# Weight conversion, softmax denominators and tile buffers: a change of operand places, engines and order in an attention and MLP kernel

## The chip, the cores and the metric

The kernel runs on one core of one Trainium2 chip. The metric is the device time of one execution in microseconds. The core's engines work side by side, each through its own instructions in order: TensorE (PE in the profile; PEld are its weight loads), VectorE (DVE), ScalarE (ACT), GpSimd (POOL), and SyncE (SP), which here only issues DMA transfers. Engines wait for each other by semaphores. SBUF is the on-chip memory that the engines read and write; PSUM is the smaller memory into which TensorE writes its products, and which DVE and ACT can read and write too.

## The reference: what is computed

Attention over a sliding window of 128 with a distance bias per head, then two matrix products with the mish activation between them:

```python
B, H, S, D = 8, 8, 576, 64
scores = q @ k.T / sqrt(D)
scores = where((rel >= 0) & (rel < 128), scores - slope[h] * |rel|, -1e9)   # rel = i - j
attn = exp(scores - max(scores))
attn = attn / (sum(attn) + 1e-9)
x = (attn @ v).transpose(0, 2, 1, 3).reshape(B * S, H * D)      # 4608 x 512
h = x @ w_in                                                    # 4608 x 2048
out = (h * tanh(log1p(exp(h)))) @ w_out                         # 4608 x 512
```

The inputs q, k and v are float32. The two weight matrices reach the chip as the bits of float64 numbers, as pairs of 32-bit words.

## The kernel before, in words

**Batches and stages.** The 4608 tokens are worked in nine chunks of 512: chunk c < 8 is the first 512 tokens of batch c, and the ninth chunk gathers the last 64 tokens of every batch. Ahead of the loop comes the attention of batch 0 with the conversion of three weight tiles (the "first attention"). Then each turn c of the loop has two stages. Stage 1 computes h = x @ w_in in eight steps j of 24 products (`first`, 192 products `h` in all) and applies mish on ACT (`mish`, tile `g`). Stage 2 computes g @ w_out (`second`, products `po`) and, mixed with it, the attention of the next batch.

**Precision.** Each operand of the two large products is split into an upper and a lower part in fp32r, and three products are made of them. `split_x` splits x (ACT copies, DVE subtracts), `parts` splits g into tile `gg` (ACT copies, POOL subtracts), and `convert_w` splits the weights into `si` and `so`.

**Weight conversion.** There are 16 weight tiles: eight of w_in (`wi`) and eight of w_out (`wo`), each 128 x 2048 words, in the order of the list `conv`. A conversion has four steps. `scaled` (line 147): ACT scales the upper words, read as float32, into tile `t` (`ti`, `to` in the profile); where `sign` is set ACT also replaces the upper words by their sign. `joined` (line 159): DVE shifts and joins the bits. Where `sign` is set, two operations of 1024 elements write into `t`, and POOL multiplies by the sign; otherwise three operations of 1024 elements write the float32 value over the upper words. `upper` (line 194): ACT copies the value into the upper part. `lower` (line 198): POOL subtracts. In the run before, three weights are converted with the sign in the first attention, ten without it in stage 1 of turn 0, and three with it in stage 2 of turn 0.

**Attention.** A batch has four pairs of heads, and each pair two units (`unit`, line 260) of two blocks of 128 rows, and one last unit (`last_unit`, line 365) for the last 64 rows, with an `l` behind the pair's number in names. A unit makes scores `s` on PE into PSUM; DVE adds the bias and ACT takes the exponential, with sums in `sm` (tile `pz`); `fold` adds the two halves on POOL and takes the reciprocal of the sums on DVE; `scale` multiplies by it; PE transposes the weights into PSUM; DVE multiplies them by the triangular `masks`; PE multiplies with v (`o`). In a last unit, the DVE does fold and scaling too, and the result is copied to tile `xo` and stored to `xs` in DRAM through SP's queue, for the ninth chunk. The tile pool `at` has two buffers of a tile unless told otherwise, and so `xo` has two.

**Order.** Every engine works in program order (`InOrder`, lines 20 to 32; the profile therefore shows line 30 for nearly all instructions). The program order is written by hand: each step has a due time, steps of a stage are sorted by it and written out. Stage steps have due times in units of j, attention steps in units of one unit's number k, and a conversion has one due time for each of its four steps (lines 560 to 597). SP's queue holds, in this order, the loads of batch 0, the loads of sixteen halves of `wi` and fourteen of `wo`, and then the stores of `xo` and the loads of batch 1.

Of the kernel before, what the change touches and what calls it, by code (L numbers as in the profile page):

```python
# [35 lines left out]
def attention_mish_mlp(  # L36
# [38 lines left out]

    nb = const.tile([P, H, 2 * WINDOW], BF16, tag="nb", name="nb")
# [10 lines left out]


    masks = const.tile([P, 2, P], BF16, tag="masks", name="masks")
    make_lower_triangular(nc, masks[:, 0, :], diag=False)  # L90
    make_upper_triangular(nc, masks[:, 1, :])
# [5 lines left out]
    zero = const.tile([P, 1], U32, tag="zero", name="zero")  # L97
    pool.memset(zero, 0)
# [7 lines left out]
    def big(name, dtype):  # L106
        return wts.tile([P, 2048], dtype, tag="w", name=name, bufs=2 * NJ + NF // 4)
# [29 lines left out]
    def convert_w(kind, j, sign):  # L137
# [9 lines left out]
        def scaled():  # L147
            st["w"] = split[(kind, j)] = big(f"s{kind}{j}", F32R)
            if not bits:
                return  # L150
            st["t"] = t = ff.tile([P, 1024], F32, tag="gg", name=f"t{kind}{j}", bufs=3)
            for a, raw in enumerate(parts_):
                val = raw[:, 1::2].bitcast(F32)

                act.activation(t[:, a * n : (a + 1) * n], val, AF.Copy, scale=2.0**-112)
                if sign:
                    act.activation(val, val, AF.Sign)

        def joined():
            if not bits:  # L160
                return
            for a, raw in enumerate(parts_):
                low, high = raw[:, 0::2], raw[:, 1::2]
                t = st["t"][:, a * n : (a + 1) * n]
                tb = t.bitcast(U32)
                out_ = tb if sign else high
# [8 lines left out]
                if sign:
                    val = high.bitcast(F32)
                    pool.tensor_tensor(out=val, in0=t, in1=val, op=ALU.mult)
                else:
                    dve.scalar_tensor_tensor(
                        out=high, in0=tb, scalar=0x80000000, in1=high, op0=ALU.bitwise_and,  # L180
                        op1=ALU.bitwise_or,
                    )
# [19 lines left out]
        return scaled, joined, upper, lower  # L202
# [57 lines left out]
    def unit(b, p, half):  # L260
# [43 lines left out]
        def fold():  # L304
            sm, pz = st["sm"], st["pz"]
            two = pz if half else pz[:, 1:4:2]
            pool.tensor_tensor(out=two[:, :, :P], in0=two[:, :, :P], in1=two[:, :, P:], op=ALU.add)
            dve.scalar_tensor_tensor(
                out=sm, in0=sm, scalar=1e-9, in1=sm, op0=ALU.add, op1=ALU.max
            )  # L310
            dve.reciprocal(sm, sm)

        def scale():
            (pool if b == 0 else dve).tensor_tensor(
                out=st["pz"][:, :, :P], in0=st["pz"][:, :, :P],
                in1=st["sm"].rearrange("p (c n) -> p c n", n=1).to_broadcast([P, 4, P]), op=ALU.mult,
            )
# [47 lines left out]
    def last_unit(b, p):  # L365
# [45 lines left out]
        def values():  # L411
# [8 lines left out]
            xo = at.tile([P, LEFT], F32, tag="xo", name=f"xo{name}")  # L420
# [73 lines left out]
    po = {}  # L494
# [171 lines left out]
```

## Time and profile before

| what | us |
|---|---|
| median of 3 runs | 1073.17 (1072.72 to 1073.31) |
| the profiled execution's own time | 1073.7 |
| its span, first to last instruction | 1072.0 |
| first attention, 0 to | 83.6 |
| stage 1 of turn 0 | 83.6 to 139.2 |
| stage 2 of turn 0 | 139.2 to 225.8 |
| turn 1 (both stages) | 225.8 to 337.1 |
| PE busy, whole span | 1007.2 (94%) |
| DVE, ACT, POOL busy | 433.4, 389.1, 325.1 |

Rows of the profile name an instruction as "output tile <- input tiles", with the shape, partitions x elements; a number in brackets at the end of a row is the idle time of the engine ahead of it, and what ended that idle time. A matmul row gives rows*columns of the array, then the moving shape. The granted clock is the share of full TensorE speed that the profile records in a stretch.

### The profile page before, as it was taken

The numbers are of one execution on the slowest core, as the hardware profiler recorded it, in microseconds if no ns is written. First come the engines' busy times: TensorE is split into PE (matmuls) and PEld (weight loads), VectorE is DVE, ScalarE is ACT, GpSimd is POOL, SyncE is SP. The second block draws the span as 40 slices with busy tenths as digits, with TensorE's granted clock in tenths as the row PEclk, the third lists the DMA queues.
The fourth block names the chain that finished last, engine by engine and source line by source line (L and its number), as shares of the span: only waits on it lengthen the run. The fifth ranks groups of instructions, "written<-read, shape, count | busy, mean of one in ns | idle before, by whom it ended". The sixth has DMA issues, their size and how long they took to land.

```text
span 1072.0 us, 14004 instructions
## 1 busy us (share of the span) xinstructions
PE 1007.2 (94%) x5280; PEld 792.4 (74%) x5280; DVE 433.4 (40%) x1114; ACT 389.1 (36%) x903; POOL 325.1 (30%) x263
## 2 busy tenths in 40 slices
PE   5639867999999999999999999999999999999998
PEld 3427655788777877787778777877788778888886
DVE  4668987710663056304740275017600771010000
ACT  3435564512542154314431443235323452231121
POOL 3335567310341044203420333024401440041042
PEclk9989889999999999999999999999999999999999
DMA  8940011210122003200320022002200201010001
GB/s 271 398 158 1 0 63 36 86 37 1 53 65 67 1 26 92 67 1 25 90 68 1 24 73 65 23 2 70 82 31 1 61 33 41 1 40 20 1 1 40
DMA packets 52131, 59.30 MB, mean 55 GB/s; under 512 B 13024, under 2 KB 32608, under 8 KB 52064
## 3 DMA queue, kind: packets, MB, share of 16 engines
q1 hardware_dynamic: 50880, 57.69, 16.7%
q8 instruction: 42, 0.69, 0.3%
q10 hardware_dynamic: 1184, 0.72, 0.2%
q14 instruction: 25, 0.20, 0.1%
HBM read 47.91 MB, written 10.49 MB: 54 GB/s over the span
## 4 chain that ended last, share of the span: by engine, by line
PE 85%; DVE 7%; issue 4%; POOL 2%; ACT 1%; DMA 1%; POOLq 0%; ACTq 0%; DVEq 0%
PE po L30 37%; PE h L30 33%; PE s L30 9%; PE o L30 5%; DVE wo L30 2%; DVE wi L30 2%; DVE pz L30 1%; DVE to L30 1%; POOL pz L30 1%; DMA nb<-in_relb_dram 1%; ACT pz L30 1%; POOL so L30 0%; DVE pz_2l L30 0%; POOL gg L30 0%; DMA first<-in_k_dram 0%
## 5 line engine op out<-in xcount | busy, mean ns | idle before, releaser
L30 PE MATMUL po<-so,gg 128*128 128x512 f32 x1728 | 433.1, 401 | 0.2 <-POOL gg L30 0.2
L30 PE MATMUL h<-x,si 128*128 128x512 f32 x1728 | 398.0, 392 | 4.8 <-ACT g L30 4.8
L30 POOL TENSOR_TENSOR gg<-g,gg 128x512 fp32r<-128x512 f32 x144 | 188.6, 1313 | 652.3 <-ACT gg L30 584.9
L30 PEld LDWEIGHTS h<-x,si 128*128 128x128 f32 x1728 | 326.8, 189 | 73.8 <-ACT g L30 5.5
L30 PEld LDWEIGHTS po<-so,gg 128*128 128x128 f32 x1728 | 317.2, 190 | 74.1 <-ACT x L30 6.6
L30 DVE CUSTOM_DVE_ANT_0 pz<-s,nb 128x256 f32<-128x256 f32 (+1 forms) x256 | 84.6, 386 | 303.2 <-PE s L30 293.6
L30 ACT ACTIVATE pz<-pz,mx 128x256 f32<-128x256 f32 (+1 forms) x256 | 120.4, 471 | 180.8 <-DVE mx L30 180.8
L30 ACT ACTIVATE g<-h 128x1024 f32<-128x1024 f32 x72 | 73.9, 1026 | 267.4 <-PE h L30 267.4
L30 ACT ACTIVATE gg<-g 128x512 fp32r<-128x512 f32 x144 | 88.5, 621 | 46.6 <-PE po L30 46.6
L30 DVE TENSOR_TENSOR pz<-s,masks 128x1024 f32<-128x1024 f32 x64 | 78.3, 1223 | 24.9 <-PE s L30 24.9
L30 DVE TENSOR_TENSOR pz<-pz,sm 128x512 f32<-128x512 f32 x56 | 55.7, 994 | 59.9 <-POOL pz L30 59.9
L30 POOL TENSOR_TENSOR pz<-pz 128x256 f32<-128x256 f32 x64 | 64.3, 1005 | 26.3 <-ACT pz L30 26.3
L30 PE MATMUL s<-ident,pz 128*128 128x128 f32 x256 | 43.4, 297 | 24.3 <-POOL pz L30 14.1
L30 PE MATMUL s<-qk 64*128 64x128 f32 (+1 forms) x448 | 58.4, 380 | 3.8 <-ACT g L30 3.8
L30 PEld LDWEIGHTS s<-ident,pz 128*128 128x128 f32 x256 | 34.2, 152 | 35.6 <-POOL pz L30 16.3
L30 DVE COPY ob<-po 128x512 f32<-128x512 f32 x18 | 12.4, 692 | 117.5 <-PE po L30 117.5
L30 PE MATMUL o<-pz,va 128*64 128x128 f32 (+1 forms) x560 | 54.9, 325 | 1.6 <-DVE pz L30 1.6
L30 PEld LDWEIGHTS o<-pz,va 128*64 128x64 f32 x560 | 33.3, 136 | 29.6 <-issue 12.0
L30 ACT ACTIVATE x<-o 128x512 fp32r<-128x512 f32 x32 | 19.1, 596 | 85.9 <-PE o L30 85.9
L30 ACT ACTIVATION_READ_ACCUMULATOR pz<-pz,mx 128x1 f32 x256 | 47.9, 187 | 0.0
L30 PEld LDWEIGHTS s<-qk 64*128 64x128 f32 x448 | 34.4, 188 | 15.0 <-issue 8.2
L30 DVE SCALAR_TENSOR_TENSOR sm<-sm 128x4 f32<-128x4 f32 x64 | 36.3, 568 | 12.5 <-ACT pz L30 12.5
(121 smaller groups left out, 521.5 us busy)
## 6 DMA issues: line engine op xcount, KB each, us to landing
wi<-in_moe_w_in_dram SPq DMA_DIRECT2D x16, 512.0 KB, 10.1
wo<-in_moe_w_out_dram SPq DMA_DIRECT2D x16, 512.0 KB, 10.2
out_dram<-ob SPq DMA_DIRECT2D x32, 256.0 KB, 2.0
qk<-in_q_dram SPq DMA_DIRECT2D x28, 288.0 KB, 3.7
qk<-in_k_dram SPq DMA_DIRECT2D x28, 288.0 KB, 4.0
va<-in_v_dram SPq DMA_DIRECT2D x28, 256.0 KB, 2.9
first<-in_q_dram SPq DMA_DIRECT2D x4, 288.0 KB, 3.9
first<-in_k_dram SPq DMA_DIRECT2D x4, 288.0 KB, 4.3
```

The costliest lines, as they stand in the source:

```text
L30: return self.tc.keep_in_program_order(method(*args, **kwargs))
```

## The change

It has eight parts. (1) `masks` is built first on POOL. (2) The tile `zero` is gone: in conversions with the sign (now called `early`) the first DVE operation is a tensor_scalar on one tensor in SBUF, where it was a scalar_tensor_tensor with the broadcast zero. (3) Conversions of stage 1 are done in two halves of 512: ACT writes the scaled words into PSUM (tiles `t` under the tags po0 and po1), DVE shifts them from PSUM to PSUM (tiles `u`, tags w and o), and two more DVE operations have one operand in SBUF and one in PSUM. That is six DVE operations of 512 for one weight, where there were three of 1024. (4) Three, nine and four weights are converted in the first attention, stage 1 and stage 2, where it was three, ten and three; due times are new. (5) Denominators of a unit are written into a free part of its scores in PSUM, and `scale` runs on DVE for batch 0 too, where it ran on POOL. (6) In a last unit the add moves from DVE to POOL and the scaling from DVE to ACT. (7) `xo` has four buffers. (8) Products of the masks with themselves, 128 x 256 in bf16, are written to a PSUM tile `idle` that nothing reads: 18 ahead of the first attention, four and eight in each of its units.

```diff
-    def convert_w(kind, j, sign):
+    def convert_w(kind, j, early):
...
+            if not early:
+                t = st[a] = ps.tile([P, 512], F32, tag=f"po{a}", name=f"t{kind}{j}_{a}")
+                act.activation(t, halves[a][:, 1::2].bitcast(F32), AF.Copy, scale=2.0**-112)
+                return
...
+            if not early:
+                low, high, tb = halves[a][:, 0::2], halves[a][:, 1::2], st[a].bitcast(U32)
+                u = ps.tile([P, 512], F32, tag=("w", "o")[a], name=f"u{kind}{j}_{a}").bitcast(U32)
+                dve.tensor_scalar(
+                    out=u, in0=tb, scalar1=3, scalar2=None, op0=ALU.logical_shift_left
+                )
+                dve.scalar_tensor_tensor(
+                    out=high, in0=low, scalar=29, in1=u, op0=ALU.logical_shift_right,
+                    op1=ALU.bitwise_or,
+                )
+                dve.scalar_tensor_tensor(
+                    out=high, in0=tb, scalar=0x80000000, in1=high, op0=ALU.bitwise_and,
+                    op1=ALU.bitwise_or,
+                )
+                return
...
-                dve.scalar_tensor_tensor(
-                    out=out_, in0=tb, scalar=3, in1=zero.to_broadcast([P, n]), op0=ALU.logical_shift_left,
+                dve.tensor_scalar(
+                    out=tb, in0=tb, scalar1=3, scalar2=None, op0=ALU.logical_shift_left
+                )
...
-            dve.scalar_tensor_tensor(
-                out=sm, in0=sm, scalar=1e-9, in1=sm, op0=ALU.add, op1=ALU.max
-            )
-            dve.reciprocal(sm, sm)
+
+            r = st["r"] = st["s"][:, 1, :4]
+            dve.tensor_scalar(out=r, in0=sm, scalar1=1e-9, scalar2=None, op0=ALU.add)
+            dve.reciprocal(r, r)
 
         def scale():
-            (pool if b == 0 else dve).tensor_tensor(
+            dve.tensor_tensor(
...
-            dve.scalar_tensor_tensor(
-                out=sm, in0=sm, scalar=1e-9, in1=sm, op0=ALU.add, op1=ALU.max
-            )
-            dve.reciprocal(sm, sm)
-            dve.tensor_tensor(out=pz[:, :64], in0=pz[:, :64], in1=pz[:, P:], op=ALU.add)
-            dve.tensor_scalar(out=pz[:, :P], in0=pz[:, :P], scalar1=sm, scalar2=None, op0=ALU.mult)
+            pool.tensor_tensor(out=pz[:, :64], in0=pz[:, :64], in1=pz[:, P:], op=ALU.add)
+            r = st["s"][:, 1, 4:5]
+            dve.tensor_scalar(out=r, in0=sm, scalar1=1e-9, scalar2=None, op0=ALU.add)
+            dve.reciprocal(sm, r)
+            act.activation(pz[:, :P], pz[:, :P], AF.Copy, scale=sm)
...
-            xo = at.tile([P, LEFT], F32, tag="xo", name=f"xo{name}")
+            xo = at.tile([P, LEFT], F32, tag="xo", name=f"xo{name}", bufs=4)
...
+    idle = ps.tile([P, 512], F32, tag="po0", name="idle")
+
+    def busy(n):
+        for _ in range(n):
+            pe.matmul(
+                idle[:, : 2 * P], lhsT=masks[:, 0, :], rhs=masks.rearrange("p u n -> p (u n)"),
+                start=True, stop=True,
+            )
+
+    def stages(*times):
+        t, d, u, low = times
+        return t, t + 0.01, d, d + 0.01, u, low
+
     early = attention(0) + converting(
-        conv[:3], [(4.3, 4.8, 5.6, 5.7), (5.5, 6.35, 7.1, 7.2), (7.0, 8.1, 8.7, 8.8)], True
+        conv[:3],
+        [stages(4.3, 4.85, 5.6, 5.7), stages(5.5, 6.4, 7.1, 7.2), stages(7.0, 8.1, 8.7, 8.8)], True,
     )
+    for k in range(2 * NP):
+        early += [(k + 0.015, lambda: busy(4)), (k + 1.35, lambda: busy(8))]
...
+    busy(18)
     run(early)
...
-            starts = [-0.5 + 0.78 * n for n in range(10)]
+            starts = [-0.5 + 0.84 * n for n in range(9)]
             steps += converting(
-                conv[3:13], [(t, t + 0.3, t + 1.1, t + 1.15) for t in starts], False
+                conv[3:12], [(t, t + 0.42, t + 0.3, t + 0.72, t + 1.15, t + 1.2) for t in starts], False
             )
...
-                conv[13:], [(0.5, 1.5, 3.5, 3.6), (2.5, 3.6, 5.5, 5.6), (6.0, 7.0, 9.0, 9.1)], True
+                conv[12:],
+                [
+                    stages(0.3, 1.2, 2.8, 2.9), stages(2.0, 3.0, 4.8, 4.9),
+                    stages(4.0, 5.0, 6.8, 6.9), stages(7.0, 8.0, 10.0, 10.1),
+                ],
+                True,
             )
```

Where the instructions stand: DVE at the start of stage 1 of turn 0, just behind the last unit of the first attention (`pz_3_1` is pair 3, half 1; the number behind a name tells buffers apart). Before:

```order
L30 TENSOR_TENSOR pz_3_1_508<-s_3_1_491,masks 128x2x4x128
L30 TENSOR_TENSOR x_3_575<-o_3_537,x_3_575 128x512
L30 SCALAR_TENSOR_TENSOR wi_148<-ti_597,zero 128x1024
L30 SCALAR_TENSOR_TENSOR wi_148<-wi_148 128x1024
L30 SCALAR_TENSOR_TENSOR wi_148<-ti_597,wi_148 128x1024
```

The same place with the change:

```order
L30 TENSOR_TENSOR pz_3_1_605<-s_3_1_584,masks 128x2x4x128
L30 TENSOR_TENSOR x_3_688<-o_3_642,x_3_688 128x512
L30 TENSOR_SCALAR ui_0_712<-ti_0_710 128x512
L30 SCALAR_TENSOR_TENSOR wi_146<-wi_146,ui_0_712 128x512
L30 SCALAR_TENSOR_TENSOR wi_146<-ti_0_710,wi_146 128x512
L30 TENSOR_SCALAR ui_1_718<-ti_1_716 128x512
L30 SCALAR_TENSOR_TENSOR wi_146<-wi_146,ui_1_718 128x512
L30 SCALAR_TENSOR_TENSOR wi_146<-ti_1_716,wi_146 128x512
```

Three operations of 1024 have become twice three of 512; `ti` and `ui` are in PSUM now.

ACT in the first attention, around the last unit of pair 2 (`pz_2l`); `ti` and `wi` belong to the first weight converted there. Before:

```order
L30 ACTIVATE ti_366<-wi_139 128x1024
L30 ACTIVATE wi_139<-wi_139 128x1024
L30 ACTIVATE pz_2l,sm_2l<-pz_2l,mx_2l 128x192
L30 ACTIVATE x_1_396<-o_1_330 128x512
L30 ACTIVATE pz_2_1_401,sm_2_1_400<-pz_2_1_401,mx_2_1_399 128x256 x4
```

With the change:

```order
L30 ACTIVATE ti_427<-wi_137 128x1024
L30 ACTIVATE wi_137<-wi_137 128x1024
L30 ACTIVATE pz_2l,sm_2l<-pz_2l,mx_2l 128x192
L30 ACTIVATE pz_2l<-pz_2l,sm_2l 128x128
L30 ACTIVATE x_1_469<-o_1_387 128x512
L30 ACTIVATE pz_2_1_474,sm_2_1_473<-pz_2_1_474,mx_2_1_472 128x256 x4
```

The scaling of the last unit stands ahead of the copy of x and of the next unit's exponentials. It needs POOL's add and DVE's reciprocal.

POOL in stage 2 of turn 0, where weights of w_out are converted beside the attention of batch 1 (`pz` rows are its folds, `gg` the lower parts of g). Before:

```order
L30 TENSOR_TENSOR gg_0_4_969<-g_2_756,gg_0_4_969 128x512
L30 TENSOR_TENSOR pz_0_1_954<-pz_0_1_954 128x4x128
L30 TENSOR_TENSOR so_932<-wo_181,so_932 128x2x512
L30 TENSOR_TENSOR gg_0_5_1002<-g_2_756,gg_0_5_1002 128x512
L30 TENSOR_TENSOR wo_0_869<-to_1012,wo_0_869 128x512
L30 TENSOR_TENSOR wo_1_870<-to_1012,wo_1_870 128x512
L30 TENSOR_TENSOR gg_0_6_1065<-g_3_833,gg_0_6_1065 128x512
L30 TENSOR_TENSOR pz_1_0_1039<-pz_1_0_1039 128x2x128
```

With the change:

```order
L30 TENSOR_TENSOR gg_0_4_1137<-g_2_911,gg_0_4_1137 128x512
L30 TENSOR_TENSOR so_1097<-wo_176,so_1097 128x2x512
L30 TENSOR_TENSOR wo_179<-to_1151,wo_179 128x1024
L30 TENSOR_TENSOR pz_0_1_1127<-pz_0_1_1127 128x4x128
L30 TENSOR_TENSOR gg_0_5_1177<-g_2_911,gg_0_5_1177 128x512
L30 TENSOR_TENSOR so_1150<-wo_179,so_1150 128x2x512
L30 TENSOR_TENSOR gg_0_6_1236<-g_3_997,gg_0_6_1236 128x512
L30 TENSOR_TENSOR wo_0_1037<-to_1222,wo_0_1037 128x512
L30 TENSOR_TENSOR wo_1_1038<-to_1222,wo_1_1038 128x512
L30 TENSOR_TENSOR pz_1_0_1208<-pz_1_0_1208 128x2x128
L30 TENSOR_TENSOR pz_1l<-pz_1l 128x64
```

Between the fold of the second unit (`pz_0_1`) and that of the third (`pz_1_0`) there is a whole weight's pair of operations more ahead of it, and the add of the last unit has joined.

More of the change, by code (lines that the diff above doesn't have):

```diff
@@ L74, in attention_mish_mlp @@
     nc.scalar.preload_act_table_set("exp_and_others")
+    masks = const.tile([P, 2, P], BF16, tag="masks", name="masks")
+    make_lower_triangular(nc, masks[:, 0, :], diag=False)
+    make_upper_triangular(nc, masks[:, 1, :])
     nb = const.tile([P, H, 2 * WINDOW], BF16, tag="nb", name="nb")
@@ L86, in attention_mish_mlp @@
         nc.gpsimd.memset(t[64:P], 0.0)
-    masks = const.tile([P, 2, P], BF16, tag="masks", name="masks")
-    make_lower_triangular(nc, masks[:, 0, :], diag=False)
-    make_upper_triangular(nc, masks[:, 1, :])
     xs = dram.tile([NCC, P, CH], F32, tag="xs", name="xs")
@@ L96, in attention_mish_mlp @@
     )
-    zero = const.tile([P, 1], U32, tag="zero", name="zero")
-    pool.memset(zero, 0)
     bits = w_in.dtype != F32
@@ L145, in convert_w, with scaled @@
         st = {}
-        def scaled():
-            st["w"] = split[(kind, j)] = big(f"s{kind}{j}", F32R)
+        def scaled(a):
+            if a == 0:
+                st["w"] = split[(kind, j)] = big(f"s{kind}{j}", F32R)
             if not bits:
+                return
[3 more added lines that the diff above has]
+                return
+            if a:
                 return
@@ L155, in scaled, with joined @@
                 act.activation(t[:, a * n : (a + 1) * n], val, AF.Copy, scale=2.0**-112)
-                if sign:
-                    act.activation(val, val, AF.Sign)
-        def joined():
+                act.activation(val, val, AF.Sign)
+        def joined(a):
             if not bits:
+                return
+            if not early:
[12 more added lines that the diff above has]
+                )
+                return
+            if a:
                 return
@@ L165, in joined @@
                 tb = t.bitcast(U32)
-                out_ = tb if sign else high
+                dve.tensor_scalar(
+                    out=tb, in0=tb, scalar1=3, scalar2=None, op0=ALU.logical_shift_left
+                )
                 dve.scalar_tensor_tensor(
-                    out=out_, in0=tb, scalar=3, in1=zero.to_broadcast([P, n]), op0=ALU.logical_shift_left,
+                    out=tb, in0=low, scalar=29, in1=tb, op0=ALU.logical_shift_right,
                     op1=ALU.bitwise_or,
                 )
-                dve.scalar_tensor_tensor(
-                    out=out_, in0=low, scalar=29, in1=out_, op0=ALU.logical_shift_right,
-                    op1=ALU.bitwise_or,
-                )
[L175 to L178, printed above, removed]
-                    dve.scalar_tensor_tensor(
-                        out=high, in0=tb, scalar=0x80000000, in1=high, op0=ALU.bitwise_and,
-                        op1=ALU.bitwise_or,
-                    )
+                val = high.bitcast(F32)
+                pool.tensor_tensor(out=val, in0=t, in1=val, op=ALU.mult)
         def values_and_places():
@@ L200, in lower @@
                 pool.tensor_tensor(out=low, in0=val, in1=up.bitcast(F32), op=ALU.subtract)
-        return scaled, joined, upper, lower
+        return (
+            lambda: scaled(0), lambda: scaled(1), lambda: joined(0), lambda: joined(1), upper, lower
+        )
     def w_part(kind, j, part, c):
@@ L307, in fold @@
             pool.tensor_tensor(out=two[:, :, :P], in0=two[:, :, :P], in1=two[:, :, P:], op=ALU.add)
-            dve.scalar_tensor_tensor(
-                out=sm, in0=sm, scalar=1e-9, in1=sm, op0=ALU.add, op1=ALU.max
-            )
-            dve.reciprocal(sm, sm)
+            r = st["r"] = st["s"][:, 1, :4]
+            dve.tensor_scalar(out=r, in0=sm, scalar1=1e-9, scalar2=None, op0=ALU.add)
+            dve.reciprocal(r, r)
         def scale():
-            (pool if b == 0 else dve).tensor_tensor(
+            dve.tensor_tensor(
                 out=st["pz"][:, :, :P], in0=st["pz"][:, :, :P],
-                in1=st["sm"].rearrange("p (c n) -> p c n", n=1).to_broadcast([P, 4, P]), op=ALU.mult,
+                in1=st["r"].rearrange("p (c n) -> p c n", n=1).to_broadcast([P, 4, P]), op=ALU.mult,
             )
@@ L557, in converting @@
         return steps
+    idle = ps.tile([P, 512], F32, tag="po0", name="idle")
[4 more added lines that the diff above has]
+                start=True, stop=True,
+            )
+    def stages(*times):
+        t, d, u, low = times
+        return t, t + 0.01, d, d + 0.01, u, low
     early = attention(0) + converting(
-        conv[:3], [(4.3, 4.8, 5.6, 5.7), (5.5, 6.35, 7.1, 7.2), (7.0, 8.1, 8.7, 8.8)], True
-    )
+        conv[:3],
+        [stages(4.3, 4.85, 5.6, 5.7), stages(5.5, 6.4, 7.1, 7.2), stages(7.0, 8.1, 8.7, 8.8)], True,
+    )
+    for k in range(2 * NP):
+        early += [(k + 0.015, lambda: busy(4)), (k + 1.35, lambda: busy(8))]
     early += [
```

2 lines of the change are left out of this document (removed).

## The prediction

> **What bounds the kernel now.** I read the page first, then the table by stage (start and end; length, then busy time and instructions of PE, PEld, DVE, ACT, POOL; granted clock, DMA share, GB/s), then the chain of waits.
>
> ```profile
> span 1072.0 us, 14004 instructions
> 0.00:83.60 83.60, 43.99 (x224) 29.77 (x224) 51.25 (x129) 29.12 (x85) 32.91 (x44) 0.92 0.76 265
> 83.60:139.20 55.60, 47.06 (x201) 37.65 (x200) 52.50 (x30) 30.38 (x30) 30.38 (x10) 0.93 0.06 19
> 139.20:225.80 86.60, 74.53 (x421) 55.85 (x422) 61.06 (x144) 42.75 (x108) 49.83 (x34) 0.92 0.17 51
> 225.80:337.10 111.30, 111.30 (x614) 87.62 (x613) 43.74 (x134) 40.80 (x104) 28.48 (x24) 1.00 0.15 45
> 225.82 43.52 PE h L30 x192
> ```
>
> The fourth row is batch 1: TensorE (PE) is busy in all of its 111.30 us, 43.52 of them the 192 h products (0.2267 each), which leaves 67.7 for stage 2. Later batches are alike, and the change takes no product out of them. The three stretches ahead, 225.8 us together, have PE idle or at a low clock. The forecast is made there.
>
> **First attention (A).** Three things cost time here: a store, a slow clock, the converting of weights. First the store, in the timelines of PE, SP's queue and VectorE (DVE): start, duration, and in brackets the idle time before.
>
> ```profile
> 49.68 2.75 PE L30 MATMUL s<-first 64*128 64x128 f32 x12
> 52.39 0.33 SPq L30 DMA_DIRECT2D xs<-xo_0l  x1
> 61.56 0.22 DVE L30 COPY xo_2l<-pt_2l 128x64 f32<-128x64 f32 x1 [12.24 <-DMA xs<-xo_0l]
> 61.70 0.28 DVE L30 CUSTOM_DVE_ANT_0 pz<-s,nb 128x128 f32<-128x128 f32 x1
> ```
>
> The third last-block unit copies into `xo`, whose two buffers are taken until the first store has landed. That store is issued at 52.39, because SP's queue has the weight loads ahead of it, and lands at 61.5. DVE stands 12.24 us. With four buffers (one per pair) the copy doesn't wait. Next late are the scores s, which end at 49.68 + 2.75 = 52.43: DVE's next step starts there instead of at 61.70. Gain 61.70 − 52.45 = **9.25**.
>
> Second the clock. The same shapes in first attention and in later stages, then PE's load by 3.5 us:
>
> ```profile
> 23.81 1.97 PE L30 MATMUL o<-pz,first 128*64 128x128 f32 x12 [1.57 <-DVE pz L30]
> 176.24 1.09 PE L30 MATMUL o<-pz,va 128*64 128x128 f32 x12 [1.55 <-DVE pz L30]
> 25.71 2.08 PE L30 MATMUL s<-first 64*128 64x256 f32 x8
> 149.56 1.13 PE L30 MATMUL s<-qk 64*128 64x256 f32 x8
> 66.50:70.00 3.50, 1.23 (x8) 1.00 0.14 44
> 70.00:73.50 3.50, 1.33 (x5) 0.60 0.00 0
> 80.50:84.00 3.50, 3.50 (x13) 0.50 0.00 0
> 84.00:87.50 3.50, 3.50 (x23) 0.95 0.00 0
> ```
>
> Twelve o take 1.97 instead of 1.09, eight s 2.08 instead of 1.13: half speed through the first attention, although the table grants 1.00 as late as 66.50; there I trust the durations. Where the table does show the half clock, it comes after slices with little PE work (1.23 of 3.50) and goes after a full one.
>
> So the unread products ought to buy the full clock. I estimate one at 256/512 × 0.2267 = 0.11 us (bounds 0.11 to a weight load's share, some 0.19): the eight after the transposes make 0.9 to 1.5 us inside PE's wait of 1.55 while DVE masks the weights, the four after the scores stand beside the exponentials. Bounds: nothing, and half of all 43.99 busy us. In my replay of the chain with warm durations, an interval in which o (1.97 − 1.09 = .88) and s (2.08 − 1.13 = .95) both stand on the chain gains 1.83 and up to .1 of transposes: 1.93, 1.88 and 1.85 in three; one with s alone .93; the start, where a few transposes count, .66. In the rest DVE and ACT cover PE. Together **7.25**.
>
> By the Trainium skill, page "TensorE: Matmul & The Clock Gate", section Part 1, PE gets its full clock after one busy window of about 3.4 us and loses it after one idle window. This case's rows agree (full after 80.50:84.00, half after 66.50:70.00). But by the same rule a start with a gap of 3.4 us is cold again, and the 18 products ahead of the attention could end that early:
>
> ```profile
> 6.79 4.76 PE L30 MATMUL s<-first 64*128 64x128 f32 x20 [6.79 <-DMA first<-in_k_dram]
> 2.78 0.29 POOL masks.py:66 TENSOR_SCALAR_AFFINE_SELECT masks<-masks 128x128 bf16<-128x128 bf16 x1
> ```
>
> The masks, built by 3.07 now and 1 us sooner after, release these products; 18 cold ones at twice 0.11 end near 6, and real scores start at 6.8. The gap is short, so I count the start as warm.
>
> Third, two conversion steps lose. Last-block scaling moves from DVE to ACT, its add to POOL, where a conversion product of the same time can be ahead:
>
> ```profile
> 50.99 2.40 POOL L30 TENSOR_TENSOR si<-wi,si 128x1024 fp32r<-128x1024 f32 x1 [1.91 <-ACT si L30]
> ```
>
> ACT, in order, holds the copies of x and the exponentials of the next unit behind that scaling. Bounds 0 and two POOL operations, 4.8; in the replay one wait of 2.07, with .62 regained as shorter joins: +1.45. The eight unread products ahead of the last h and o add .65 (8 × 0.11 less what stands in a wait; 1.8 if cold). **A = −9.25 − 7.25 + 1.45 + .65 = −14.4**: first attention ends at 69.2.
>
> **Stage 1 of the first batch (B).** Ten conversions run here. POOL and DVE timelines, the groups (count, then busy us and mean ns) of the third and second join operations, PE's waits:
>
> ```profile
> 126.77 3.36 POOL L30 TENSOR_TENSOR so<-wo,so 128x1024 fp32r<-128x1024 f32 x1 [2.41 <-ACT so L30]
> L30 DVE SCALAR_TENSOR_TENSOR wo<-to,wo 128x1024 uint32<-128x1024 uint32 x4 | 13.3, 3335 | 0.1
> L30 DVE SCALAR_TENSOR_TENSOR wo<-wo 128x1024 uint32<-128x1024 uint32 x5 | 6.1, 1227 | 0.2
> 116.09 7.29 PE L30 MATMUL h<-x,si 128*128 128x512 f32 x19 [4.77 <-ACT g L30]
> 139.17 1.65 PE L30 MATMUL s<-qk 64*128 64x128 f32 x8 [3.77 <-ACT g L30]
> ```
>
> Both two-input operations in SBUF, DVE's third and POOL's, stretch when they meet (3.34 against 1.23, 3.36 against the 2.40 above): on DVE 2 × 1.23 + 3.34 = 5.8 a weight. ACT's mish waits in that queue, and PE for it: 4.77, then 3.77. The prices for the new code, none of which has two SBUF inputs:
>
> ```profile
> L30 DVE TENSOR_TENSOR x<-o,x 128x512 fp32r<-128x512 f32 x4 | 2.8, 688 | 4.2 <-ACT x L30 4.2
> L30 DVE TENSOR_TENSOR pz<-s,masks 128x1024 f32<-128x1024 f32 x8 | 9.8, 1220 | 2.4 <-PE s L30 2.4
> L30 ACT ACTIVATE to<-wo 128x512 f32<-128x512 f32 x2 | 1.3, 650 | 0.0
> 83.53 1.14 ACT L30 ACTIVATE si<-wi 128x1024 fp32r<-128x1024 f32 x1 [8.30 <-POOL wi L30]
> L30 ACT ACTIVATE g<-h 128x1024 f32<-128x1024 f32 x72 | 73.9, 1026 | 267.4 <-PE h L30 267.4
> ```
>
> A PSUM-and-SBUF operation of 512 takes .69, and of 1024 it took 1.22 beside POOL as well. Per weight DVE spends 6 × .69 = 4.1 (bounds 6 × .6 and 6 × 1.2), POOL 2.40, ACT 2 × .65 + 1.14 = 2.4. Nine weights stand in eight steps of 24 h, 5.44 us each: DVE 4.6, POOL 2.7, ACT 2.8 + 1.03 = 3.8 a step. PE is the longest, so it should run through: 186 h still ahead × .2267 = 42.2, the last o 1.4, and .3 at the change of engines: 43.9. **B = 43.9 − 55.6 = −11.7.** At DVE's upper bound (8.1 a step) nothing would be gained.
>
> **Stage 2 of the first batch (C).** The waits of PE for transposed weights, and the late mish:
>
> ```profile
> 143.86 1.01 ACT L30 ACTIVATE g<-h 128x1024 f32<-128x1024 f32 x1
> 156.55 1.12 PE L30 MATMUL s<-ident,pz 128*128 128x128 f32 x4 [4.27 <-DVE pz L30]
> 169.79 1.09 PE L30 MATMUL s<-ident,pz 128*128 128x128 f32 x4 [4.34 <-DVE xo_0l L30]
> 181.61 0.64 PE L30 MATMUL s<-ident,pz 128*128 128x128 f32 x4 [1.63 <-DVE pz L30]
> ```
>
> 10.2 us of waits lie here. A fourth weight moves in: two POOL operations of 2.40 and three of ACT of 1.14, 8.2 us on the engines that end these waits. Against it, the last mish, which now ends 5.7 us into the stage, is due about 1 us in: −4.7. Also, denominators in PSUM take DVE's scaling off the shared inputs. If all of the added work shows, +8; if the waits go instead, −8. I take the difference 8.2 − 4.7, rounded down for the shorter joins: **C = +3**.
>
> **Steady batches: 0.** Here the last-block add (now POOL) stands behind a gg subtraction, and ACT behind it:
>
> ```profile
> 194.22 1.48 POOL L30 TENSOR_TENSOR gg<-g,gg 128x512 fp32r<-128x512 f32 x1 [1.24 <-ACT gg L30]
> 197.77 1.23 DVE L30 TENSOR_TENSOR pz<-s,masks 128x1024 f32<-128x1024 f32 x1 [0.39 <-PE s L30]
> 200.52 0.87 PE L30 MATMUL o<-pz,va 128*64 128x256 f32 x8
> ```
>
> In the third pair ACT's copy of x and what follows slip by up to 1.5 us. DVE's masking would end at 200.15 by my shift of these rows; PE needs it at 200.52. A slack of .37, thin, but enough: PE stays the bound and the cost is hidden by its products. In the other pairs nothing slips.
>
> **Sum**, against the profiled run of 1073.7 (span and 1.7 around it; the median of the runs is 0.5 lower): 1073.7 − 14.4 − 11.7 + 3 + 0 = **1050.6**.
>
> **Rivals.**
> 1. *PE stays cold in the first attention.* For it: PE is cold there today, and half of the load would be transposes and gaps. Against: the products fill PE by about 12 × 0.11 in each unit. Then 7.25 are not gained, and eight cold products, 1.8, exceed the wait of 1.57 by .24 in each of seven units, +1.7: 1059.6.
> 2. *Stage 1 keeps its pace*, DVE's operations slowed in spite of PSUM (8.1 a step): B = 0, 1062. Against: the masking at 1.22 beside POOL.
> 3. *The early joins are blocked by POOL.* Their shift is now an operation with one SBUF tensor. Such a one did suffer:
>
> ```profile
> 13.88 0.28 DVE L30 TENSOR_SCALAR pz_0l<-pz_0l,sm_0l 128x128 f32<-128x128 f32 x1
> 275.17 1.33 DVE L30 TENSOR_SCALAR pz_0l<-pz_0l,sm_0l 128x128 f32<-128x128 f32 x1
> ```
>
> 1.33 − .28 = 1.05 for each of seven weights, 7.4: 1058. The Trainium skill, page "SBUF — State Buffer", section "Who interferes with whom", names this operation as one that can take the pair of ports shared with GpSimd for its whole length. The trace agrees with it in the second row.
>
> 4. *Stage 2's waits go* (C = −8): 1040.
> 5. *Slower.* ACT's wait on POOL in last-block units delays PE in every steady batch: at worst 1.5 us in 4 units of 7 batches, 42, gives 1093. It decides the sign from 23.1 / 28 = .83 us a unit on. Against: .37 of slack in one pair, much more in three.
>
> **Chances.** Forecast .62 (own range 1043 to 1058); cold PE .10; old pace .07; blocked joins .07; stage 2 hidden .10; slower .04. The range 1040 to 1064 takes in all but the slow rival and the tails of the others. A change of 0.2% (2.1 us) is about what a measurement of this kernel can tell from none: faster .95, same .01, slower .04.
>
> **What would show it.** No idle time at `xo_2l`; twelve o in about 1.1 us before 60 us (cold: 2.0); first attention ending near 69; stage 1 in 44 us without waits for g, joins of .7; transposes of stage 2 at 13, 30 and 43 us from its start; PE busy in all of batch 1, at 111.3 us. If batch 1 is longer, the fifth rival holds, and the forecast fails there.

## The result and the profile after

The changed kernel takes 1048.47 us (median of four runs, 1048.3 to 1051.22) against 1073.24 before; the ratio is 0.9775 (95% interval 0.9758 to 0.9792). The forecast was 1050.6. The profiled execution took 1048.58, its span is 1046.9. The table by stage of the changed kernel, with the same columns as before (start and end; length, then busy time and instructions of PE, PEld, DVE, ACT, POOL; granted clock, DMA share, GB/s):

```profile
0.00:69.10 69.10, 45.58 (x338) 32.82 (x338) 39.18 (x129) 31.26 (x89) 24.83 (x39) 0.88 0.92 321
69.10:112.65 43.55, 43.55 (x201) 35.50 (x200) 36.64 (x55) 30.19 (x39) 25.27 (x12) 1.00 0.00 1
112.65:200.50 87.85, 74.46 (x421) 55.47 (x422) 45.38 (x136) 45.39 (x112) 48.70 (x37) 0.92 0.20 62
200.50:311.60 111.10, 111.10 (x613) 87.43 (x613) 36.41 (x126) 42.18 (x108) 29.31 (x28) 1.00 0.15 44
```

The first attention and stage 1 lie where the forecast put them: the first attention is 14.5 shorter (83.59 to 69.05, the starts of the last o; forecast 14.4) and stage 1 of turn 0 is 12.1 shorter (11.7). Stage 2 is 1.3 longer and not 3. A steady batch takes 111.1 (111.3 before), and from turn 1 to the end both kernels take the same 846 us.

**The store.** DVE's timeline around the third last unit:

```profile
42.69 0.69 DVE L30 TENSOR_TENSOR pz<-pz,s 128x512 f32<-128x512 f32 x1 [0.76 <-POOL pz L30]
43.39 0.23 DVE L30 COPY xo_2l<-pt_2l 128x64 f32<-128x64 f32 x1
45.54 0.29 DVE L30 CUSTOM_DVE_ANT_0 pz<-s,nb 128x128 f32<-128x128 f32 x1 [1.93 <-PE s L30]
```

The copy into `xo_2l` has no idle time in front; what is late next is PE's scores, as forecast.

**The clock.** "Warm" is PE at its full clock, "cold" at half of it. PE's timeline, warm and cold places, and then the table of all engines by 3.5 us (same columns as above):

```profile
21.06 1.09 PE L30 MATMUL o<-pz,first 128*64 128x128 f32 x12 [0.68 <-DVE pz L30]
41.36 1.55 PE L30 MATMUL o<-pz,first 128*64 128x256 f32 x8 [3.39 <-DVE pz L30]
47.93 1.09 PE L30 MATMUL o<-pz,first 128*64 128x128 f32 x12 [0.68 <-DVE pz L30]
...
38.50:42.00 3.50, 0.64 (x4) 0.45 (x6) 3.40 (x13) 2.83 (x9) 0.62 (x1) 0.90 1.05 396
42.00:45.50 3.50, 3.50 (x30) 2.56 (x27) 0.92 (x2) 2.44 (x3) 1.55 (x2) 0.61 1.02 407
56.00:59.50 3.50, 0.00 (x0) 0.00 (x0) 3.21 (x11) 2.40 (x7) 0.00 (x0) 0.50 1.03 400
```

Twelve o take 1.09 and no longer 1.97. Where DVE and ACT keep PE waiting for over 3 us (a slice with 0.64 busy, one with none), the clock falls to half all the same: the unread products of a unit are issued in one go and don't bridge that. The Trainium skill, page "TensorE: Matmul & The Clock Gate", section Part 1, says that the array is at half its clock after an idle window of about 3.4 us. The trace of this run agrees (8 o took 1.55 behind the wait of 3.39). Run e4 below differs from it: there the granted clock fell from 1.00 to .50 near 23.7 and 33.9 us, though from PE's first scores up to then no wait was longer than 1.99, so a shorter pause can be enough.

**The conversions in stage 1.** Groups of DVE (those of the w_in weights; w_out is alike), then of POOL and ACT, in 69.1 to 112.65 (count, then busy us and mean ns):

```profile
L30 DVE SCALAR_TENSOR_TENSOR wi<-ti,wi 128x512 uint32<-128x512 uint32 x10 | 6.9, 693 | 0.3
L30 DVE TENSOR_SCALAR ui<-ti 128x512 uint32<-128x512 uint32 x10 | 6.9, 691 | 0.5 <-ACT ti L30 0.5
L30 DVE SCALAR_TENSOR_TENSOR wi<-wi,ui 128x512 uint32<-128x512 uint32 x10 | 6.9, 688 | 0.3
```

```profile
L30 POOL TENSOR_TENSOR si<-wi,si 128x1024 fp32r<-128x1024 f32 x6 | 14.7, 2453 | 13.2 <-ACT si L30 13.2
L30 ACT ACTIVATE g<-h 128x1024 f32<-128x1024 f32 x7 | 7.1, 1017 | 0.0
```

All three kinds take .69, the forecast's price, and POOL takes 2.45, no longer 3.36. PE has no wait in this stage: 43.55 of 43.55 us busy.

### The profile page after: what moved, and what is told of

Same layout as the page of the kernel before. It is cut to its first block, busy times and chain, and to the rows that moved or that the text cites. A ratio compares the mean times of both kernels' runs of the same rounds, so it can differ in the third digit from the quotient of the medians.

```text
span 1046.9 us, 14298 instructions
## 1 busy us (share of the span) xinstructions
PE 1005.4 (96%) x5394; PEld 792.9 (76%) x5394; DVE 345.6 (33%) x1084; ACT 402.1 (38%) x945; POOL 315.8 (30%) x287
## 4 chain that ended last, share of the span: by engine, by line
PE 88%; POOL 3%; issue 1%; ACT 1%; DVE 1%; POOLq 0%
PE h L30 38%; PE po L30 36%; PE s L30 8%; PE o L30 5%; POOL wo L30 1%; POOL so L30 1%; DVE pz L30 1%; DVE to L30 1%; POOL pz L30 0%; ACT to L30 0%; POOL gg L30 0%; ACT so L30 0%; PE pt_3l L30 0%; ACT pz L30 0%; PE pt_2l L30 0%
## 5 line engine op out<-in xcount | busy, mean ns | idle before, releaser
L30 POOL TENSOR_TENSOR gg<-g,gg 128x512 fp32r<-128x512 f32 x144 | 185.3, 1290 | 649.9 <-ACT gg L30 547.2
L30 PEld LDWEIGHTS h<-x,si 128*128 128x128 f32 x1728 | 324.9, 188 | 67.8 <-ACT g L30 0.2
L30 DVE TENSOR_TENSOR pz<-pz,s 128x512 f32<-128x512 f32 x64 | 43.9, 685 | 104.3 <-POOL pz L30 104.3
L30 PE MATMUL s<-ident,pz 128*128 128x128 f32 x256 | 40.1, 280 | 21.2 <-DVE pz L30 11.4
L30 PEld LDWEIGHTS s<-ident,pz 128*128 128x128 f32 x256 | 31.8, 143 | 31.0 <-issue 12.1
L30 PEld LDWEIGHTS s<-qk 64*128 64x128 f32 x448 | 33.9, 186 | 11.2 <-issue 8.2
L30 DVE TENSOR_TENSOR x<-o,x 128x512 fp32r<-128x512 f32 x32 | 22.1, 692 | 58.0 <-ACT x L30 58.0
```

The source lines that it names most:

```text
L30: return self.tc.keep_in_program_order(method(*args, **kwargs))
```

## The experiments

Each kernel's stretches are measured alike: A is the start of the last o of the first attention, B runs from there to the first scores of stage 2, C from there to turn 1.

| kernel | median us | A | B | C |
|---|---|---|---|---|
| before | 1073.24 | 83.59 | 55.58 | 86.65 |
| changed | 1048.47 | 69.05 | 43.52 | 87.91 |
| e1_xo4 | 1064.34 | 74.63 | 55.71 | 86.79 |
| e2_products | 1074.35 | 86.09 | 55.26 | 86.59 |
| e3_both | 1061.32 | 71.09 | 54.92 | 86.71 |
| e4_no_products | 1051.08 | 70.21 | 44.20 | 88.20 |
| e5_join_sbuf | 1058.67 | 68.43 | 51.72 | 89.58 |
| e6_conv_3_10_3 | 1043.65 | 69.17 | 43.55 | 83.12 |
| e7_last_on_dve | 1044.25 | 64.27 | 43.71 | 87.46 |
| e8_den_sbuf | 1050.05 | 69.42 | 43.55 | 89.17 |
| e9_e6_and_e7 | 1039.97 | 65.67 | 43.55 | 83.13 |
| e10_scale_pool | 1053.54 | 72.17 | 43.55 | 89.21 |
| e11_conv_2_11_3 | 1037.76 | 59.84 | 45.39 | 84.68 |
| e12_products_3_units | 1039.65 | 64.39 | 44.21 | 82.93 |

The start of the real work moves from one profile to the next (DVE's first masking at 15.00 in e9 and at 13.72 in e12, whose programs are the same up to there), so a difference in A of 1 us says little by itself; where it matters, A is counted from the first masking on. An interval below is the time from one unit's masking on DVE to the next unit's; there are seven of them. The kernel before had medians of 1073.24 to 1073.78 in the four sets of runs, so medians of different sets compare to about half a microsecond.

### Single parts put into the kernel before: e1, e2, e3

```diff
-            xo = at.tile([P, LEFT], F32, tag="xo", name=f"xo{name}")
+            xo = at.tile([P, LEFT], F32, tag="xo", name=f"xo{name}", bufs=4)
```

> The kernel before with four xo buffers and nothing else. Theory (the copy into xo waits for a store that lands at 61.5 behind the weight loads): the 12.24 us wait at xo_2l goes, PE's scores are next late, first attention ends about 9.25 earlier (74.3 instead of 83.6), in all 1064 us. Rival (the wait only moves, to a weight that has not landed or to a later store): first attention ends less than 3 us earlier, 1070 or more.

Measured: ratio 0.9914 (0.9897 to 0.993), A shorter by 8.96, B and C unchanged. The store is worth about what the forecast said (9.25).

e2 adds `idle`, `busy` and its calls (the diff's part 8) to the kernel before:

> The kernel before with the unread products and nothing else; xo keeps two buffers. Theory (products buy the full clock, but the store lands at 61.5 whatever comes ahead of it): twelve o take 1.09, units 1 to 4 come 5.4 us earlier, the wait at xo_2l grows by as much, and only the 1.9 us behind it show: 1071.3. Rival A (clock and store are independent): 7.25 us less, 1066. Rival B (PE stays cold or the products stand in the way): 1073 to 1076.

Measured: 1.001 (1.0001 to 1.002), no gain. DVE's wait in e2, and PE at the end of its first attention:

```profile
62.36 0.23 DVE L30 COPY xo_2l<-pt_2l 128x64 f32<-128x64 f32 x1 [18.75 <-DMA xs<-xo_0l]
```

```profile
81.68 1.91 PE L30 MATMUL idle<-masks 128*128 128x256 bf16 x8
83.25 2.91 PE L30 MATMUL h<-x,si 128*128 128x512 f32 x6
86.09 1.43 PE L30 MATMUL o<-pz,first 128*64 128x128 f32 x12
```

The wait at `xo_2l` grows from 12.24 to 18.75: what the warm clock wins ahead of the store is swallowed by it, as the theory had it. Behind the store the theory was wrong. It expected 1.9 more, but the units there take 10.2 and 8.2 with and without products, and eight cold products (1.91) stand in front of the last h and o. The number falls into rival B's range, for half of its reason: PE was not cold in units 1 to 4, but at the end the products do stand in the way.

e3 has both:

> The kernel before with four xo buffers and the unread products. Theory: the two gains add only here, 9.25 + 7.25 = 16.5 in the first attention (ends at 67.1), 1056.7 in all. Rival (with both gone the conversions or the weight loads become the bound of the first attention): 10 to 12 us, 1062.

Measured: 0.9886 (0.9871 to 0.99), 1061.32. Against e1, the products win 3.5 us in A: 4.4 up to the fourth unit, nothing from there to the seventh (the intervals are 8.7 and 10.2 in both), and .8 lost at the end. The forecast had 7.25 for the clock. The rival's number came true, and its mechanism for the later units: in the sixth interval of e3 POOL's scaling stands behind a conversion's subtraction of 2.40, and DVE waits 3.45 for the transposed weights that need it.

### The changed kernel without the products: e4

```diff
-        early += [(k + 0.015, lambda: busy(4)), (k + 1.35, lambda: busy(8))]
-    busy(18)
```

> The changed kernel without the unread products. Theory: PE is cold again in the first attention (twelve o 1.97 instead of 1.09); 7.25 us lost, .65 regained at its end: first attention ends near 75.7 instead of 69.1, 1055 in all. Rival (the clock is set by the real work, since the attention runs denser now): twelve o stay at 1.1 in most units, 1047 to 1049.

Measured: 1051.08 (1050.37 to 1052.23), a loss of only 2.6 where 6.6 was expected; the ranges of the two kernels overlap. PE's timeline in e4:

```profile
22.93 1.31 PE L30 MATMUL o<-pz,first 128*64 128x128 f32 x12 [1.99 <-DVE pz L30]
28.95 0.87 PE L30 MATMUL o<-pz,first 128*64 128x256 f32 x8 [1.60 <-DVE pz L30]
31.36 0.60 PE L30 MATMUL s<-ident,pz 128*128 128x128 f32 x4
33.95 1.97 PE L30 MATMUL o<-pz,first 128*64 128x128 f32 x12 [1.99 <-DVE pz L30]
50.49 1.56 PE L30 MATMUL o<-pz,first 128*64 128x128 f32 x12 [1.99 <-DVE pz L30]
```

Between theory and rival: the clock comes and goes without the products too (.87 and 1.31 beside 1.97; transposes at .60 just ahead of the o at 1.97). What the products change is PE's wait ahead of twelve o: 1.99 without them, .68 with them. The first two intervals between maskings take 6.97 and 6.02 in place of 5.01 and 5.46; in the other five the products change .15 at most. At the end e4 gains 1.38 back: from the last masking to the last o it takes 1.82, the changed kernel 3.20 with eight cold products in between. So A loses only 1.16, and B .68, where h begins with a colder PE.

### Stage 1 joined in SBUF again: e5

```diff
-                t = st[a] = ps.tile([P, 512], F32, tag=f"po{a}", name=f"t{kind}{j}_{a}")
...
+                    t = st["t"] = ff.tile([P, 1024], F32, tag="gg", name=f"t{kind}{j}", bufs=3)
...
-                dve.tensor_scalar(
-                    out=u, in0=tb, scalar1=3, scalar2=None, op0=ALU.logical_shift_left
-                )
...
+                    out=high, in0=tb, scalar=3, in1=zero.to_broadcast([P, 1024]),
+                    op0=ALU.logical_shift_left, op1=ALU.bitwise_or,
+                )
```

The edit goes back from six DVE operations of 512 to three of 1024 as well, and brings `zero` back.

> The changed kernel with the nine conversions of stage 1 joined in SBUF as before: three DVE operations of 1024 a weight, two of them with two SBUF inputs, tile t in SBUF; numbers, due times and the rest as in the changed kernel. Theory (two inputs from SBUF make DVE and POOL stretch each other): the third operation takes 3.3 again beside POOL at 3.36, 5.8 us a weight, nine weights 52; stage 1 takes 52 to 55 instead of 43.55, 1057 to 1060 in all. Rival (what helped in stage 1 is that there are nine weights and not ten, and their order): stage 1 under 47, 1052 at most.

Measured: 1058.67, 10.2 more than the changed kernel; B 51.72. DVE's and POOL's groups in stage 1 of e5:

```profile
L30 DVE SCALAR_TENSOR_TENSOR wo<-to,wo 128x1024 uint32<-128x1024 uint32 x4 | 13.3, 3334 | 0.1
```

```profile
L30 POOL TENSOR_TENSOR so<-wo,so 128x1024 fp32r<-128x1024 f32 x3 | 10.1, 3353 | 7.2 <-ACT so L30 7.2
```

Both stretch again (3.33 and 3.35), and PE waits 4.7 for the mish once more; the rival's "under 47" is out. With nine weights the way through PSUM is worth 8.2 us of stage 1; place of the operands and halving were not tried apart. The other 3.9 to the kernel before go with its tenth weight and its due times. They don't show that ten are too many: with operands in PSUM ten weights take 43.55 too (e6 below), so at ten the way through PSUM is worth all of the 12.0. The Trainium skill, page "SBUF — State Buffer", section "Who interferes with whom", says that a DVE instruction with two SBUF inputs contends with a GpSimd one that reads SBUF, and that one with at most one SBUF input, outside the 2-port modes that the page names, doesn't. The pair of runs agrees (3.33 for 1024 elements against .69 for 512).

### Ten weights in stage 1: e6

```diff
-            starts = [-0.5 + 0.84 * n for n in range(9)]
+            starts = [-0.5 + 0.78 * n for n in range(10)]
...
-                conv[12:],
+                conv[13:],
```

and the three due times of before for stage 2.

> The changed kernel with three, ten and three weights in first attention, stage 1 and stage 2, at the due times of before. Theory (stage 1 has room: DVE 10 x 4.1 / 8 = 5.1 a step of 5.44; stage 2 loses two POOL operations of 2.4 ahead of the second unit's fold): stage 1 stays within 0.7 of 43.55, stage 2 takes 84 to 85 instead of 87.85, 1045 in all. Rival (stage 1 is at its limit with nine): stage 1 46 to 49, and the sum is 1048 to 1051.

Measured: 1043.65 (ratio to before 0.9722, 0.9707 to 0.9736), 4.8 less than the changed kernel, all of it in C; B is 43.55, still without a wait, so the rival is out. POOL in stage 2 of the changed kernel, and PE behind it:

```profile
135.39 2.39 POOL L30 TENSOR_TENSOR so<-wo,so 128x1024 fp32r<-128x1024 f32 x1 [2.31 <-ACT so L30]
137.75 2.37 POOL L30 TENSOR_TENSOR wo<-to,wo 128x1024 f32<-128x1024 f32 x1
140.07 1.26 POOL L30 TENSOR_TENSOR pz<-pz 128x512 f32<-128x512 f32 x1
```

```profile
125.37 0.66 PE L30 MATMUL s<-ident,pz 128*128 128x128 f32 x4 [3.10 <-DVE pz L30]
142.20 1.08 PE L30 MATMUL s<-ident,pz 128*128 128x128 f32 x4 [7.21 <-DVE xo_0l L30]
```

and PE in the same place of e6:

```profile
127.30 1.11 PE L30 MATMUL s<-ident,pz 128*128 128x128 f32 x4 [4.89 <-DVE pz L30]
138.08 0.63 PE L30 MATMUL s<-ident,pz 128*128 128x128 f32 x4 [1.80 <-DVE xo_0l L30]
```

The second unit's fold stands behind two more POOL operations of 2.4, and PE's wait there grew from 4.34 (before) to 7.21. The row names the DVE copy as the releaser because it came last; the chain goes back to POOL. In e6 that wait is 1.80. The gain of 4.8 is that of one weight less and of the due times of before together.

### The last unit on DVE again: e7

```diff
-            pool.tensor_tensor(out=pz[:, :64], in0=pz[:, :64], in1=pz[:, P:], op=ALU.add)
...
-            act.activation(pz[:, :P], pz[:, :P], AF.Copy, scale=sm)
+            dve.tensor_tensor(out=pz[:, :64], in0=pz[:, :64], in1=pz[:, P:], op=ALU.add)
+            dve.tensor_scalar(out=pz[:, :P], in0=pz[:, :P], scalar1=sm, scalar2=None, op0=ALU.mult)
```

> The changed kernel with the last unit's add and scaling back on DVE (two SBUF inputs again), its sum still in PSUM. Theory (ACT's wait for POOL behind a weight's product holds the copies of x): waits of ACT for the add of pair 2 and 3 in the first attention (3.2 and 2.6) go, first attention ends 1.5 to 4 us earlier; steady batches do not change (111.1); 1045 to 1047. Rival (DVE's add waits for the same POOL product at the shared inputs, as its 2.42 for 64 elements did before the change): no gain, 1048 to 1049.

Measured: 1044.25 (0.9729, 0.9715 to 0.9744), 4.2 less than the changed kernel. From the first masking to the last o it takes 50.4 us (13.85 to 64.27) against 54.3 (14.78 to 69.05), 3.9 less. ACT of the changed kernel, then DVE and POOL of e7, at the third pair:

```profile
37.19 0.40 ACT L30 ACTIVATE pz_2l<-pz_2l,sm_2l 128x128 f32<-128x128 f32 x1 [3.19 <-POOL pz_2l L30]
37.50 0.58 ACT L30 ACTIVATE x<-o 128x512 fp32r<-128x512 f32 x1
```

```profile
34.45 2.39 DVE L30 TENSOR_TENSOR pz_2l<-pz_2l 128x64 f32<-128x64 f32 x1
37.68 0.68 DVE L30 TENSOR_TENSOR x<-o,x 128x512 fp32r<-128x512 f32 x1
34.40 2.37 POOL L30 TENSOR_TENSOR wi<-ti,wi 128x1024 f32<-128x1024 f32 x1 [2.31 <-ACT x L30]
```

The rival's mechanism is there: DVE's add of 64 elements takes 2.39, as long as POOL's product beside it. But ACT isn't caught in it: in e7 it has copied x before POOL's product begins (the product waited for ACT's x), and in the changed kernel only at 37.50. All the same the fifth interval gains only .26. The sixth (5.00 against 6.57) and the seventh (9.58 against 11.61) pay. In the sixth it is PE's clock; DVE's wait for the scores of that unit is 1.93 in the changed kernel (shown above) and .40 in e7, and their products take, in the changed kernel and then in e7:

```profile
43.27 2.23 PE L30 MATMUL s<-first 64*128 64x128 f32 x12
41.96 1.54 PE L30 MATMUL s<-first 64*128 64x128 f32 x12
```

In e7 the transposes and the unread products of the fifth unit run at 37.9 to 40.9, right ahead of its o, and PE is warm by then; in the changed kernel they run at 35.4 to 38.0 and the wait of 3.39 follows. In the seventh interval it is ACT's copy of x, for which DVE waits 2.69 in the changed kernel:

```profile
56.29 0.69 DVE L30 TENSOR_TENSOR x<-o,x 128x512 fp32r<-128x512 f32 x1 [2.69 <-ACT x L30]
```

### Where denominators and scaling stand: e8, e10

e8 computes the denominators of units in SBUF (the old two lines of `fold`), the scaling stays on DVE; e10 is e8 with `(pool if b == 0 else dve)` in `scale`.

> The changed kernel with the units' denominators in SBUF, so that DVE's scaling has two SBUF inputs again (on DVE in all batches). Theory (hidden in steady batches, where PE is always busy; on the path only in the first attention and in stage 2 of turn 0): scaling 0.69 becomes about 1.0 to 1.2, 0.3 to 1.5 us lost in each of the two stretches, 1049 to 1051, steady batches 111.1. Rival (these inputs are what holds PE in stage 2): stage 2 of turn 0 loses 4 us or more, 1053.

> The changed kernel with denominators in SBUF and the scaling of batch 0 on POOL, as before the change; to be compared with the same kernel with the scaling on DVE (first attention 69.4). Theory (what the forecast put down to the clock is for a good part the scaling: POOL's 1.16 became DVE's 0.69, and POOL's conversion products no longer stand ahead of it): first attention ends at 72 to 74, 1052 to 1055 in all. Rival (the scaling was hidden, the clock alone shortened the chain): first attention below 70.5, 1051 at most.

Measured: e8 1050.05 (1048.34 to 1053.13), which can't be told from the changed kernel by these runs; by its profile .4 in A and 1.3 in C, and nothing in the steady batch (111.24), though the scaling rose from .69 to .99. e10 1053.54: A 2.75 longer than in e8, B and C equal. POOL's group in the first attention of e10, and PE in its sixth unit:

```profile
L30 POOL TENSOR_TENSOR pz<-pz,sm 128x512 f32<-128x512 f32 x8 | 8.6, 1079 | 0.8 <-DVE xo_1l L30 0.4 <-DVE sm L30 0.4
```

```profile
47.90 1.11 PE L30 MATMUL s<-ident,pz 128*128 128x128 f32 x4 [3.72 <-POOL pz L30]
```

Nearly all of the 2.75 lies in that one interval (9.23 against 6.55), where POOL has a conversion's subtraction (44.45 to 46.85) ahead of the scaling (46.81). So the moved scaling, for which the forecast had no term of its own, was worth about as much as the products.

### Together, and further: e9, e11, e12

e9 joins the edits of e6 and e7.

> The changed kernel with three, ten and three conversions and with the last unit's add and scaling on DVE. Theory (two parts of the change each cost time, in different stretches: the fourth weight in stage 2, the last unit's way over POOL and ACT in the first attention): the gains add, 1048.5 - 4.8 - 4.2 = 1039.5; first attention ends near 64.4, stage 2 takes near 83. Rival (with POOL freed in stage 2 the last units there want DVE, and one gain hides the other): 1042 to 1044.

Measured: 1039.97, ratio 0.9684 (0.9671 to 0.9698). The two gains add. e11 converts two weights in the first attention and eleven in stage 1:

```diff
-        conv[:3],
-        [stages(4.3, 4.85, 5.6, 5.7), stages(5.5, 6.4, 7.1, 7.2), stages(7.0, 8.1, 8.7, 8.8)], True,
+        conv[:2],
+        [stages(4.3, 4.85, 5.6, 5.7), stages(7.0, 8.1, 8.7, 8.8)], True,
...
-            starts = [-0.5 + 0.78 * n for n in range(10)]
+            starts = [-0.5 + 0.71 * n for n in range(11)]
```

> As the kernel with 3, 10 and 3 weights and the last unit on DVE, with 2, 11 and 3 weights. Theory (a weight converted in the first attention costs its chain some 4.5; stage 1 has DVE work for 11 x 4.15 = 45.7 beside PE's 43.5, so up to 3 show at its end): 1.5 to 4 us less than that kernel, near 1037. Rival (stage 1 is full at ten, ACT's mish comes late and PE waits again): equal or up to 4 us more, 1040 to 1044.

Measured: 1037.76, ratio 0.9664 (0.9651 to 0.9677): the fastest kernel here, 2.2 below e9 by the medians (the ranges just touch). Against e9, A falls by 5.8, and 3.4 come back: PE of e11 in stage 1 and at the first transposes of stage 2:

```profile
82.07 17.04 PE L30 MATMUL h<-x,si 128*128 128x512 f32 x72 [0.31 <-ACT g L30]
99.56 5.74 PE L30 MATMUL h<-x,si 128*128 128x512 f32 x24 [0.45 <-ACT g L30]
122.32 1.11 PE L30 MATMUL s<-ident,pz 128*128 128x128 f32 x4 [6.25 <-DVE pz L30]
```

Stage 1 is full at eleven: B is 1.84 longer than in e9. Waits for a late mish are .76 of it (.31 and .45); most of the rest is in the products themselves, .235 for one h where e9 has .229, for which the rows show no cause. The first wait of stage 2 rises to 6.25 (4.89 in e9). So a part of the rival's mechanism is there as well, at a smaller price than the gain in A.

> As the kernel with 3, 10 and 3 weights and the last unit on DVE, with the unread products in the first three units only (and the 18 ahead). Theory (the products earn their time in the first units alone; later PE waits for the conversions anyway, and the eight ahead of the last h cost up to 1.4): within 1 us of that kernel, first attention 0 to 1.4 shorter, stage 1 0 to 0.7 longer for a cold start. Rival (products keep the clock up through the whole first attention): 2 us or more longer.

Measured: 1039.65, within .4 of e9, so the products behind the third unit buy nothing that shows in the time. From the first masking to the last o both take 50.67 us (15.00 to 65.67 and 13.72 to 64.39), but that they are equal is luck: the first interval, with the same program in both, took 5.87 in e12 and 5.00 in e9. Behind the third unit the products win 1.29 in the sixth interval and lose .45 in the seventh and 1.71 between the last masking and the last o, .87 in all; B is .66 longer without them.

## Why the prediction was right, and where its terms were not

- **Store, −9.25:** right in size and mechanism, 8.96 alone (e1). It can't be counted alone, though: while it is there, what is won ahead of it is lost (e2).
- **Clock, −7.25:** the mechanism is right, the size wrong, and this is the step that failed. The products are worth 3.5 in A beside the larger `xo` (e3 against e1), and 1.2 in A and .7 in B of the changed kernel (e4). The forecast took the cold clock of the run before for what the changed order would have without products; e4 shows that this order is warm in part without them. It counted the start as warm, but the first twelve s of the changed kernel took 2.75 where warm ones take 1.54. And it counted gains in intervals where something else stands on the chain (e3). The length of A was met all the same (69.2 forecast, 69.05 measured), and that is luck: the scaling moved to DVE is worth 2.75 (e10 against e8), and the sum had no line for it. Whether the replay behind the 7.25 held that scaling can't be seen; the terms that the prediction names for it are o, s and transposes.
- **Two conversion steps, +1.45:** too small for the last unit's way over POOL and ACT, which alone costs 3.9 in A (e7; 3.8 by e9 against e6). ACT's waits for POOL's add, 3.19 and 2.60, are there as described; that the long wait of PE behind them would take its clock, 1.6 us of the 3.9, was not in the sum. It was covered by gains not counted elsewhere: the early shift fell to .69 for 1024 elements, where the replaced operation took 1.2 to 2.0. How much of A those shifts are worth alone was not tried.
- **Eight unread products ahead of the last h and o, +.65:** they run cold (1.91), and the end of A is 1.38 longer with them (e4).
- **Stage 1, −11.7:** right, −12.1, and by its reason: PE is the longest, operations of .69, and without PSUM they stretch (e5).
- **Stage 2, +3:** right in sign, +1.3. The fourth weight with its due times costs 4.8 (e6), the forecast's working had 8.2, and the denominators in PSUM give back 1.3 (e8). The last mish ends 1.1 us into the stage, as forecast, where it was 5.7; what that is worth was not tried alone.
- **Steady batches, 0:** right, 111.10 against 111.30, and PE shows no wait from turn 1 on. The rows from which the prediction took its slack of .37 (194 to 201 us) are not of a steady batch but of stage 2 of turn 0, so that slack itself wasn't measured.

The stretches of the whole add up to 25.3 less, where 23.1 was forecast; most of the difference is stage 2. Two figures of the prediction need a word: 111.30 less 43.52 is 67.8 and not 67.7, on which nothing rests, and its mark "transposes of stage 2 at 13, 30 and 43 us" came at 12.8, 29.6 and 41.6.

Of the rivals, the old pace of stage 1, the hidden stage 2 (PE's waits for the three transposes there are 12.9 in sum, 10.2 before) and the slower steady batch did not come. Cold PE came true in places only (41.3 to 44.7 and 55 to 68.6 us by the granted clock). An early join was blocked in one of eight shifts; DVE and POOL of the changed kernel in stage 2:

```profile
144.96 2.21 DVE L30 TENSOR_SCALAR to<-to 128x512 uint32<-128x512 uint32 x1 [0.41 <-ACT to L30]
147.81 0.42 DVE L30 TENSOR_SCALAR to<-to 128x512 uint32<-128x512 uint32 x1
```

```profile
144.43 2.44 POOL L30 TENSOR_TENSOR so<-wo,so 128x1024 fp32r<-128x1024 f32 x1 [1.87 <-ACT so L30]
```

The first half began .53 us after a POOL operation and ended .3 after it; the second, alone, took .42. The six shifts of 1024 took .69, but this doesn't speak against the rival's mechanism: POOL stood idle beside them, but for one that began .03 before a POOL operation ended. The one shift that began well inside a POOL operation was blocked and lost 1.8. In e7 and e9 one shift of 1024 each begins inside a POOL subtraction (45.79 in 44.25 to 46.67 in e7), and takes 1.42 and 1.14. What the rival had wrong is how often the two meet.

## What to carry to other kernels

A replay of the changed order with durations from the trace gave the lengths of three stretches to within .1, .4 and 1.7 us, the first by luck, and it doesn't tell which edit earned them; only single edits on the chip do that, and two of eight parts here cost some 4 and 5 us under a good total. Gains ahead of a fixed event (a store behind a long queue) are nothing until that event is out of the way. Before work is moved to another engine, look at what stands ahead of it in that engine's order: 64 elements cost 3.19 us of waiting, most of it behind one POOL product of 2.4.

## What the runs showed of the hardware that had not been expected

- How long PE may wait before it loses its clock was not one figure here. Twelve o behind a wait of .68 took 1.09 wherever the profiles of these runs have one. Behind a wait of 1.99 they took 1.31, 1.97 and 1.56 in one execution of e4, 1.96 and 1.38 in e1, 1.09 and 1.85 in e12. In the first attention of the kernel before, all were cold but the last (1.97 or 1.98, then 1.43). What decides behind 1.99 the runs don't show.
- A DVE shift of 1024 elements on one SBUF tensor takes .69, as long as one of 512 with an operand in PSUM, and .42 for 512; beside a POOL operation that had begun it took 2.21.
- Eight unread products of 128 x 256 in bf16 take 1.04 warm (46.22 us of the changed kernel) and 1.91 cold (64.97).
